# The end of an attention and MLP kernel: the last output tile in two PSUM banks, and half of the last squares on ScalarE

## The chip, the cores and the metric

One NeuronCore of one Trainium2 chip runs the whole program. The time is device microseconds of one execution. Three timed runs of the kernel before gave 680.88, 681.27 and 681.51 us, median 681.27 us. A separate execution was recorded by the profiler; it took 681.12 us, of which the span of the program's instructions is 679.3 us.

## The reference, cut to what matters

```python
# attention: softmax(scale * q k^T + bias(position)) v, for 4 batches, 8 heads, 576 positions, head size 64
attn_out = np.matmul(attn, v)                                  # 4 x 8 x 576 x 64
x = attn_out.transpose(0, 2, 1, 3).reshape(2304, 512)          # tokens x d_model
h = x @ w_in                                                   # 512 -> 2048
r = np.maximum(h, 0.0)
g = r * r
out = g @ w_out                                                # 2048 -> 512
```

All is float32. The change lies in the last three lines, for the last tokens that the kernel handles.

## The kernel before, in words

The attention comes first and leaves x in SBUF. The MLP follows as a list of 40 items `(n, P)`, in the order of the table `runs` (line 1299). A group n is a set of tokens; P is one of eight slices of the hidden size, 256 hidden units each. Groups 0 to 3 are the first 512 positions of one batch. Group `B` (4) holds what is left: the last 64 positions of each of the four batches, 256 tokens. It comes last, as items 32 to 39, and its products are 128 columns wide (`width[B]`).

One item goes through these functions. The loop runs item i's first half beside the second half of item i-1:

- `products` (L1416, TensorE): seven products of sums of quarters of x and w_in (Strassen's scheme), each in six matmuls of f16 parts. Four go to the PSUM tile `ha`, three to `hb`, 42 matmuls together.
- `sums` (L1430 to L1435): ScalarE scales `ha` into `s`; then VectorE puts the quarters of h together in `c`, in four operations: `c[2:4]`, `c[0:2]`, then twice `c[2:4]`, which alone needs `hb`.
- `squares` (L1452 for the late items): one VectorE operation makes max(c, 0) * c of the four quarters.
- `parts_g` (L1467, L1468): each hidden block f (0 or 1) is cut into two f16 parts. ScalarE makes `gh`, VectorE makes `gl`, the rest. Block f = 0 is `c[1]` and `c[3]`, block f = 1 is `c[0]` and `c[2]`.
- `down` (L1535, TensorE): the product with w_out. The output of group B is two tiles of 128 tokens and 512 columns, k = 0 and k = 1, each a whole PSUM bank (`y`), which adds up over all eight items. Per item, block f and tile k there are three matmuls: gh with the two parts of w_out (m = 0 and 1) and gl (m = 2). That makes 12. In the last item they are sorted by k.
- `leave` (L1498, L1501): when tile k is complete, VectorE copies it to SBUF with its scale (`o`), and two DMAs write it out, one half of the partitions (64 rows of 2 KB, one batch) from the SyncE queue, the other half from the ScalarE queue.

Each engine works through its instructions in the order in which the code issues them (`manual_schedule`); a DMA that is issued on ScalarE's queue stands among ScalarE's instructions. In tile k = 0, block 0 uses `c[3]` and block 1 uses `c[0]`; in tile k = 1 they use `c[1]` and `c[2]`. So `c[0:2]` holds one block of each of the two output tiles, and `c[2:4]` the other.

Of the kernel before, what the change touches and what calls it, by code (L numbers as in the profile page):

```python
# [10 lines left out]
F32 = mybir.dt.float32  # L11
F32R = mybir.dt.float32r
BF16 = mybir.dt.bfloat16
F16 = mybir.dt.float16
I32 = mybir.dt.int32
U32 = mybir.dt.uint32
AF = mybir.ActivationFunctionType
ALU = mybir.AluOpType
# [3 lines left out]
B, H, S, D = 4, 8, 576, 64  # L22
# [51 lines left out]
FINE = 1024.0  # L74
# [5 lines left out]
def attention_then_relu2_mlp(ctx: ExitStack, tc: tile.TileContext, q, k, v, cols, w_in, w_out, psi, xmat, dist, out):  # L80
    nc = tc.nc
    PE, DVE, ACT, POOL, SP = nc.tensor, nc.vector, nc.scalar, nc.gpsimd, nc.sync
# [668 lines left out]
    def take(x, o, n):  # L751
        o += 18 * S * x
        return area[:, o:o + n]
# [426 lines left out]
    order = [early[0], 2, 3, *early[1:]]  # L1180
# [113 lines left out]
    mlp = ctx.enter_context(tc.tile_pool(name="mlp", bufs=1, side="right", reuse_waits="tile"))  # L1294
    ph_p = ctx.enter_context(tc.tile_pool(name="ph", bufs=1, space=PSUM, reuse_waits="tile"))
    py_p = ctx.enter_context(tc.tile_pool(name="py", bufs=1, space=PSUM, reuse_waits="tile"))
# [4 lines left out]
    NI = len(items)  # L1301
    run_of = {(n, p0): r for r, (n, p0, p1) in enumerate(runs)}
    firsts = {(n, p0) for n, p0, p1 in runs}
    lasts = {(n, p1 - 1) for n, p0, p1 in runs}
# [19 lines left out]
    part_y, ready_y = {}, {}  # L1324
    c_t, g_t, y_t = {}, {}, {}
# [78 lines left out]
    def products(i):  # L1404
        n, P = items[i]
        w = width[n]
        ha = ph_p.tile([128, 4, 256], F32, name="ha", tag="ha")
        hb = ph_p.tile([128, 4, 256], F32, name="hb", tag="hb")
        for ms, h in (((2, 3, 4, 5), ha), ((1, 6, 7), hb)):
            for s, m in enumerate(ms):  # L1410
                k = 0
                for c in range(2):
                    wh, wl = (x[:, LEFT[m]] for x in w_t[4 * P + c])
                    xh, xl = (x[:, c] for x in xs_t[n, m])
                    for a, x in ((wh, xh), (wh, xl), (wl, xh)):
                        PE.matmul(h[:, s, :w], lhsT=a, rhs=x, start=(k == 0), stop=(k == 5))  # L1416
                        k += 1
        return ha, hb

    def sums(i, ha, hb):  # L1420
        n, P = items[i]
        w = width[n]
        alpha = alpha_t[n] if plain(n, P) else root[:, n:n + 1]
        if i % 2:
            c, s = (take(1, o, 1024).rearrange("p (m t) -> p m t", m=4)[:, :, :w] for o in (4480, 5504))
        elif i < NP // 2:
            c, s = (tmp_p.tile([128, 4, 256], F32, name=x, tag=x) for x in "cs")
        else:
            c, s = (xT[1][:, :, 256 * x:256 * x + w] for x in range(2))
        ACT.activation(out=s, in_=ha[:, :, :w], func=AF.Identity, scale=alpha)  # L1430
        stt = DVE.scalar_tensor_tensor
        stt(out=c[:, 2:4], in0=ha[:, 1:3, :w], scalar=alpha, in1=s[:, 0:4:3], op0=ALU.mult, op1=ALU.subtract)
        stt(out=c[:, 0:2], in0=ha[:, 2:4, :w], scalar=alpha, in1=s[:, 0:2], op0=ALU.mult, op1=ALU.add)  # L1433
        stt(out=c[:, 2:4], in0=hb[:, 0:1, :w].to_broadcast([128, 2, w]), scalar=alpha, in1=c[:, 2:4], op0=ALU.mult, op1=ALU.add)
        stt(out=c[:, 2:4], in0=hb[:, 1:3, :w], scalar=alpha, in1=c[:, 2:4], op0=ALU.mult, op1=ALU.add)  # L1435
        c_t[i] = c

    def squares(i):
        c = c_t[i]
        if i == 0:  # L1440
            for eng, f in ((DVE, 0), (ACT, 1)):
                g = c[:, 1 - f:4:2]
                if eng is DVE:
                    DVE.scalar_tensor_tensor(out=g, in0=g, scalar=0.0, in1=g, op0=ALU.max, op1=ALU.mult)
                else:
                    ACT.activation(out=g, in_=g, func=AF.Relu)
                    ACT.activation(out=g, in_=g, func=AF.Square)
        elif i < GA:
            ACT.activation(out=c, in_=c, func=AF.Relu)
            ACT.activation(out=c, in_=c, func=AF.Square)  # L1450
        else:
            DVE.scalar_tensor_tensor(out=c, in0=c, scalar=0.0, in1=c, op0=ALU.max, op1=ALU.mult)  # L1452

    def plain(n, P):
        return n < B - 1 and P < NP // 2

    def half(n, P, f):
        return not plain(n, P) and len(w_t[4 * P + 2 + f]) == 3

    def parts_g(i):  # L1460
        (n, P), c = items[i], c_t[i]
        w = width[n]
        for f in range(2):
            if half(n, P, f):
                gl, gh = (mlp.tile([128, 4, 256], F16, name=x, tag=x, bufs=2)[:, 0:2, :w] for x in ("gl", "gh"))
                g = c[:, 1 - f:4:2]
                ACT.activation(out=gh, in_=g, func=AF.Identity, scale=1.0 / FINE)  # L1467
                DVE.scalar_tensor_tensor(out=gl, in0=gh, scalar=-FINE, in1=g, op0=ALU.mult, op1=ALU.add)  # L1468
                g_t[i, f] = (gh, gl)
                continue  # L1470
            gl = mlp.tile([128, 2, 256], F32R, name="gl", tag="gl", bufs=2)[:, :, :w]
            gh = mlp.tile([128, 2, 256], F32R, name="gh", tag="gh", bufs=2)[:, :, :w]
            g = c[:, 1 - f:4:2]
            if plain(n, P):
                ACT.copy(gh, g)  # L1475
                DVE.tensor_tensor(out=gl, in0=g, in1=gh.bitcast(F32), op=ALU.subtract)
            else:
                ACT.activation(out=gh, in_=g, func=AF.Identity, scale=oscale[2])
                DVE.scalar_tensor_tensor(out=gl, in0=g, scalar=oscale[2], in1=gh.bitcast(F32), op0=ALU.mult, op1=ALU.subtract)
            g_t[i, f] = (gh, gl)  # L1480

    def pair_tile():
        return stage_p["p"].tile([128, 2, 512], F32, name="o", tag="stage", bufs=2)
# [8 lines left out]
    def leave(n, P, k):  # L1492
        y = y_t[n][k]
        j, x = divmod(k, 2)
        unit = 1.0 if plain(n, P) else beta[:, n:n + 1]
        if n == B:
            o = ready_y[j] = pair_tile()
            DVE.tensor_scalar(out=o[:, 0], in0=y, scalar1=unit, scalar2=None, op0=ALU.mult)  # L1498
            for r, queue in enumerate((SP, ACT)):
                end = S * (2 * k + r + 1)  # L1500
                queue.dma_start(out=out[end - 64:end], in_=o[64 * r:64 * r + 64, 0])  # L1501
            return
        if (n, 0) in part_y:
            o = ready_y[j]
            DVE.scalar_tensor_tensor(out=o[:, x], in0=y, scalar=unit, in1=o[:, x], op0=ALU.mult, op1=ALU.add)
        else:
            if x == 0:
                ready_y[j] = pair_tile()
            o = ready_y[j]
            ACT.activation(out=o[:, x], in_=y, func=AF.Identity, scale=unit)  # L1510
        if x == 0:
            return
        if P < NP - 1:
            ready_y[j, "dram"] = dram.tile([128, 1024], F32, name=f"py{j}")
            SP.dma_start(out=ready_y[j, "dram"], in_=o.rearrange("p x m -> p (x m)"))
        else:
            rows = out[S * n + 256 * j:S * n + 256 * j + 256].rearrange("(x p) m -> p x m", x=2)
            SP.dma_start(out=rows, in_=o)

    def down(i):  # L1520
        n, P = items[i]
        w = width[n]
        nk = w // 64
        if (n, P) in firsts:
            banks = {k: py_p.tile([128, 512], F32, name=f"y{k}") for k in (2, 3, 0, 1) if k < nk}
            y_t[n] = [banks[k] for k in range(nk)]
        order = [(f, k, m) for f in range(2) for ms in ((0, 1), (2,)) for k in range(nk) for m in ms]
        if i == NI - 1:
            order.sort(key=lambda x: x[1])
        for f, k, m in order:  # L1530
            wh, wl, *fine = w_t[4 * P + 2 + f]
            gh, gl = g_t[i, f]
            t, o = divmod(128 * k, w)
            slot = t if f else 1 - t
            PE.matmul(  # L1535
                y_t[n][k], lhsT=(gl if m == 2 else gh)[:, slot, o:o + 128], rhs=(wh, wl, *fine)[m] if fine else (wh, wl, wh)[m],
                start=((n, P) in firsts and f == 0 and m == 0), stop=((n, P) in lasts and f == 1 and m == 2),
            )
            if (n, P) in lasts and f == 1 and m == 2:
                leave(n, P, k)  # L1540
        if (n, P) in lasts and P < NP - 1:
            for j in range(2):
                part_y[n, j] = ready_y[j, "dram"]

    tmp_p = tmp_stack.enter_context(tc.tile_pool(name="tmp", bufs=1, side="right", reuse_waits="tile"))
    with tc.manual_schedule():
# [4 lines left out]
        for i in range(NI + 1):  # L1551
# [4 lines left out]
            n, P = items[min(i, NI - 1)]  # L1556
            if i:
                fetch_y(i - 1)
            if i < NI:
                ha, hb = products(i)  # L1560
# [9 lines left out]
            if i < NI:  # L1570
                sums(i, ha, hb)
# [35 lines left out]
            if i < NI and (n, P) in firsts:  # L1607
                r = run_of[n, P]
# [56 lines left out]
```

## Time and profile before

| | |
|---|---|
| timed runs, median (lowest to highest) | 681.27 us (680.88 to 681.51) |
| profiled execution / its span | 681.12 us / 679.3 us |
| TensorE matmul busy | 662.9 us, 98% |
| VectorE, ScalarE, GpSimd busy | 558.6, 484.9, 222.8 us |
| group B on TensorE, one item | 4.93 us (start to start) |
| end of the last matmul to the end of the span | 4.4 us |

Busy shares say which engine has work; what ends the program is read from the chain of waits, which goes back from the last instruction through whatever released each step. The span ends when the last output transfer has landed and the engines have met at the final barrier.

### The profile page before, as it was taken

The numbers are of one execution on the slowest core, as the hardware profiler recorded it, in microseconds if no ns is written. First come the engines' busy times: TensorE is split into PE (matmuls) and PEld (weight loads), VectorE is DVE, ScalarE is ACT, GpSimd is POOL, SyncE is SP. The second block draws the span as 40 slices with busy tenths as digits, with TensorE's granted clock in tenths as the row PEclk, the third lists the DMA queues.
The fourth block names the chain that finished last, engine by engine and source line by source line (L and its number), as shares of the span: only waits on it lengthen the run. The fifth ranks groups of instructions, "written<-read, shape, count | busy, mean of one in ns | idle before, by whom it ended". The sixth has DMA issues, their size and how long they took to land.

```text
span 679.3 us, 18939 instructions
## 1 busy us (share of the span) xinstructions
PE 662.9 (98%) x7650; PEld 509.4 (75%) x7650; DVE 558.6 (82%) x1216; ACT 484.9 (71%) x1013; POOL 222.8 (33%) x328
## 2 busy tenths in 40 slices
PE   9999999999999999899999999999999999999997
PEld 8788888887777777678888888887666666666664
DVE  7999899867779978998989879867758886798765
ACT  5779888888787999997566756775676657656321
POOL 2565545442112445455124205144212213331100
PEclk9999999999999999999999999999999999999999
DMA  6674210025073233306741040050038342633101
GB/s 200 196 248 138 94 65 3 2 88 151 11 242 104 52 115 110 104 4 220 292 171 64 32 171 32 5 229 0 1 106 316 110 153 109 226 131 121 66 2 32
DMA packets 34247, 76.67 MB, mean 113 GB/s; under 512 B 7152, under 2 KB 16496, under 8 KB 33136
## 3 DMA queue, kind: packets, MB, share of 16 engines
q1 hardware_dynamic: 34000, 75.21, 32.5%
q8 instruction: 60, 0.98, 0.6%
q14 instruction: 27, 0.22, 0.1%
q10 hardware_dynamic: 160, 0.26, 0.1%
HBM read 57.10 MB, written 18.35 MB: 111 GB/s over the span
## 4 chain that ended last, share of the span: by engine, by line
PE 71%; ACT 10%; DVE 7%; issue 4%; DMA 3%; POOL 3%; SPq 0%; ACTq 0%; POOLq 0%; DVEq 0%
PE y L1535 21%; PE sp L490 10%; PE px L623 10%; PE ha L1416 10%; PE hb L1416 7%; PE bb L430 6%; PE pp L571 4%; ACT pt L1259 3%; DMA r<-in_w_out 3%; ACT p L513 2%; DVE t L506 2%; PE pa L584 1%; POOL wa L804 1%; DVE area L906 1%; ACT o L1510 1%
## 5 line engine op out<-in xcount | busy, mean ns | idle before, releaser
L1416 PEld LDWEIGHTS <-area 128*128 128x128 f16 x1680 | 149.3, 98 | 24.4 <-issue 2.4
L1535 PE MATMUL y<-w,gh 128*128 128x512 f16 (+1 forms) x576 | 142.9, 387 | 0.7 <-ACT gh L1475 0.3
L506 DVE CUSTOM_DVE_ANT_0 t<-sp,area 128x576 f32<-128x576 f32 x144 | 103.7, 752 | 18.7 <-PE sp L490 9.6
L513 ACT ACTIVATE p<-t,negm 128x576 f32<-128x576 f32 x144 | 113.2, 799 | 1.1 <-DVE negm L506 0.9
L490 PE MATMUL sp<-k,q 64*128 64x288 f32 (+1 forms) x608 | 94.7, 427 | 2.6 <-DVE negm L506 1.6
L623 PE MATMUL px<-pt,v 128*64 128x128 f32 (+1 forms) x1600 | 92.2, 266 | 1.2 <-ACT pt L1259 1.2
L623 PEld LDWEIGHTS px<-pt,v 128*64 128x64 f32 x1600 | 79.2, 137 | 12.1 <-ACT pt L1259 8.6
L1416 PE MATMUL ha<-area 128*128 128x256 f16 (+1 forms) x816 | 84.9, 260 | 0.2 <-DVE area L1433 0.2
L445 POOL TENSOR_TENSOR area<-bt,bt 128x256 f32<-128x256 f32 x72 | 65.7, 929 | 55.6 <-DVE bt L438 55.4
L1535 PE MATMUL y<-w,gl 128*128 128x512 f16 (+1 forms) x288 | 77.0, 384 | 0.0
L490 PEld LDWEIGHTS sp<-k,q 64*128 64x128 f32 (+1 forms) x608 | 50.1, 177 | 21.1 <-issue 6.0
L1416 PE MATMUL hb<-area 128*128 128x256 f16 (+1 forms) x612 | 64.7, 260 | 0.0
L833 POOL TENSOR_TENSOR raw<-wa 128x256 f32<-128x256 f32 (+1 forms) x48 | 31.3, 679 | 88.7 <-issue 54.1
L1535 PEld LDWEIGHTS <-gh 128*128 128x128 f16 x344 | 33.1, 98 | 35.6 <-ACT gh L1467 1.1
L417 DVE TENSOR_TENSOR mask<-sdist,theta 128x1024 f16<-128x1024 f16 x81 | 58.0, 718 | 1.1 <-PE bb L430 0.8
L571 PEld LDWEIGHTS pp<-ident,p 64*128 64x128 f32 x1144 | 45.5, 139 | 13.9 <-issue 1.9
L982 ACT COPY pt<-pp 128x512 f32<-128x512 f32 (+1 forms) x76 | 37.4, 544 | 21.5 <-PE pp L571 21.4
L571 PE MATMUL pp<-ident,p 64*128 64x64 f32 x1144 | 50.1, 226 | 2.2 <-DVE raw L832 0.7
L1535 PEld LDWEIGHTS y<-w,gh 128*128 128x128 f32 x232 | 42.5, 188 | 10.2 <-ACT gh L1475 1.0
L430 PEld LDWEIGHTS <-mask 128*128 128x128 f16 x1296 | 46.3, 100 | 4.1 <-issue 1.6
L430 PE MATMUL bb<-wmov,mask 128*128 128x64 f16 x1296 | 47.3, 194 | 0.2 <-ACT pt L982 0.2
L1259 ACT COPY pt<-pp 128x512 f32<-128x512 f32 (+1 forms) x83 | 39.8, 563 | 10.8 <-PE pp L571 10.4
(231 smaller groups left out, 1103.8 us busy)
## 6 DMA issues: line engine op xcount, KB each, us to landing
raw<-in_w_in SPq DMA_DIRECT2D x20, 512.0 KB, 3.9
r<-in_w_out SPq DMA_DIRECT2D x16, 512.0 KB, 7.4
xs<-area SPq DMA_DIRECT2D x4, 1792.0 KB, 9.1
area<-in_w_in SPq DMA_DIRECT2D x12, 512.0 KB, 4.4
py<-o SPq DMA_DIRECT2D x12, 512.0 KB, 4.1
o<-py SPq DMA_DIRECT2D x12, 512.0 KB, 4.3
v<-in_v SPq DMA_DIRECT2D x16, 320.0 KB, 3.3
q<-in_q SPq DMA_DIRECT2D x32, 128.0 KB, 3.5
```

The source lines that it names most:

```text
L417: DVE.tensor_tensor(out=out, in0=win, in1=th, op=ALU.is_ge)
L430: PE.matmul(bb[:, 64 * (7 - r):64 * (8 - r)], lhsT=m[:, r], rhs=wmov[:, n], start=(n == 0), stop=(n == 1))
L445: POOL.tensor_tensor(out=dst, in0=tw, in1=sw, op=ALU.add)
L490: mm = PE.matmul(out_t[to, x, :HALF], lhsT=lhsT, rhs=rhs, start=True, stop=True)
L506: DVE.tensor_tensor_reduce(out=t.rearrange("p (x n) -> p x n", x=2), in0=sp[:, :, :HALF], in1=bias.rearrange("p (x n) -> p x n", x=2), sca ...
L513: ACT.activation(out=p[:, S * n:S * n + S], in_=t, func=AF.Exp, bias=negm[:, n:n + 1], scale=-1.0, accum_out=sums[:, 2 * ic + n:2 * ic + n ...
L571: PE.transpose(dst, p[rows, k0:k0 + 128], ident[rows, rows])
L623: PE.matmul(px[64 * h:64 * h + 64, 128 * m:128 * m + w], lhsT=vt[:, c, h], rhs=src, start=(c == 0), stop=(c == 4))
L982: ACT.copy(dst, src)
L1259: ACT.copy(*c)
L1416: PE.matmul(h[:, s, :w], lhsT=a, rhs=x, start=(k == 0), stop=(k == 5))
L1535: PE.matmul(y_t[n][k], lhsT=(gl if m == 2 else gh)[:, slot, o:o + 128], rhs=(wh, wl, *fine)[m] if fine else (wh, wl, wh)[m], start=((n, P) ...
```

## The change

Three things are changed for group B. First, tile k = 1 lies in two banks: its columns 0 to 255 in one, 256 to 511 in another, so each of its matmuls becomes two of 256 columns, in all eight items. When it is complete, VectorE copies the first half and ScalarE the second, and each half goes out as one DMA of 128 rows of 1 KB, from the SyncE and the ScalarE queue. Second, in the last item `c[0:2]` is summed first and then squared by ScalarE in two activations (Relu, Square); VectorE squares `c[2:4]` alone; `gh` and `gl` are cut in the same halves. Third, the last item's matmuls are ordered by those halves: all that use `c[0:2]` first, then the others, tile 0 before tile 1.

```diff
 def sums(i, ha, hb):
         ACT.activation(out=s, in_=ha[:, :, :w], func=AF.Identity, scale=alpha)
+        if i == NI - 1:
+            stt(out=c[:, 0:2], in0=ha[:, 2:4, :w], scalar=alpha, in1=s[:, 0:2], op0=ALU.mult, op1=ALU.add)
+            ACT.activation(out=c[:, 0:2], in_=c[:, 0:2], func=AF.Relu)
+            ACT.activation(out=c[:, 0:2], in_=c[:, 0:2], func=AF.Square)
         stt(out=c[:, 2:4], in0=ha[:, 1:3, :w], scalar=alpha, in1=s[:, 0:4:3], op0=ALU.mult, op1=ALU.subtract)
-        stt(out=c[:, 0:2], in0=ha[:, 2:4, :w], scalar=alpha, in1=s[:, 0:2], op0=ALU.mult, op1=ALU.add)
+        if i < NI - 1:
+            stt(out=c[:, 0:2], in0=ha[:, 2:4, :w], scalar=alpha, in1=s[:, 0:2], op0=ALU.mult, op1=ALU.add)
...
 def squares(i):
-        if i == 0:
+        if i == NI - 1:
+            DVE.scalar_tensor_tensor(out=c[:, 2:4], in0=c[:, 2:4], scalar=0.0, in1=c[:, 2:4], op0=ALU.max, op1=ALU.mult)
+        elif i == 0:
...
 def parts_g(i):
+        if i == NI - 1:
+            gl, gh = (mlp.tile([128, 4, 256], F16, name=x, tag=x, bufs=2)[:, :, :w] for x in ("gl", "gh"))
+            for x in (slice(0, 2), slice(2, 4)):
+                ACT.activation(out=gh[:, x], in_=c[:, x], func=AF.Identity, scale=1.0 / FINE)
+            for x in (slice(0, 2), slice(2, 4)):
+                DVE.scalar_tensor_tensor(out=gl[:, x], in0=gh[:, x], scalar=-FINE, in1=c[:, x], op0=ALU.mult, op1=ALU.add)
+            g_t[i, 0], g_t[i, 1] = ((gh[:, 1 - f:4:2], gl[:, 1 - f:4:2]) for f in range(2))
+            return
...
 def leave(n, P, k):
+        if n == B and k:
+            o = ready_y[j] = pair_tile()
+            rows = out[2 * S * k:2 * S * k + 2 * S].rearrange("(r s) m -> r s m", r=2)[:, S - 64:]
+            DVE.tensor_scalar(out=o[:, 0, :256], in0=y[0], scalar1=unit, scalar2=None, op0=ALU.mult)
+            ACT.activation(out=o[:, 0, 256:], in_=y[1], func=AF.Identity, scale=unit)
+            for x, queue in enumerate((SP, ACT)):
+                queue.dma_start(out=rows[:, :, 256 * x:256 * x + 256], in_=o[:, 0, 256 * x:256 * x + 256])
+            return
...
 def down(i):
-            banks = {k: py_p.tile([128, 512], F32, name=f"y{k}") for k in (2, 3, 0, 1) if k < nk}
+            banks = {k: py_p.tile([128, 512], F32, name=f"y{k}") for k in (2, 3, 0, 1) if k < nk + (n == B)}
             y_t[n] = [banks[k] for k in range(nk)]
+            if n == B:
+                y_t[n][1] = [banks[k][:, :256] for k in (1, 2)]
...
-            order.sort(key=lambda x: x[1])
+            order.sort(key=lambda x: (x[0] == x[1], x[2] == 2 and x[0] != x[1], x[1]))
...
+            if n == B and k:
+                for x, y in enumerate(y_t[n][k]):
+                    PE.matmul(y, lhsT=lhsT, rhs=rhs[:, 256 * x:256 * x + 256], start=start, stop=stop)
+            else:
+                PE.matmul(y_t[n][k], lhsT=lhsT, rhs=rhs, start=start, stop=stop)
```

TensorE's last instructions before the change, from the start of the last item's second half: `y_10289` is output tile 0 and `y_10290` tile 1; `w_9378` and `w_9472` are the w_out parts of the hidden blocks 0 and 1; names in brackets are the engines waited for.

```order
L1535 LDWEIGHTS gh [waits Activation_49]
L1535 MATMUL y_10289<-w_9378,gh 128x512
...
L1535 LDWEIGHTS gl [waits DVE_49]
L1535 MATMUL y_10289<-w_9472,gl 128x512
L1535 LDWEIGHTS gh
L1535 MATMUL y_10290<-w_9378,gh 128x512
...
L1535 LDWEIGHTS gl
L1535 MATMUL y_10290<-w_9472,gl 128x512
```

Tile 0 is complete when six matmuls of tile 1 are still to come.

The same place after the change, from the second half of that item on: `y_10290` is now tile 0, `y_10291` and `y_10289` are the two halves of tile 1.

```order
L1567 LDWEIGHTS gl [waits DVE_49]
L1567 MATMUL y_10290<-w_9472,gl 128x512
...
L1567 LDWEIGHTS gh [waits Activation_49]
L1567 MATMUL y_10290<-w_9378,gh 128x512
...
L1567 LDWEIGHTS gl [waits DVE_49]
L1567 MATMUL y_10290<-w_9378,gl 128x512
L1565 LDWEIGHTS gh
L1565 MATMUL y_10291<-w_9472,gh 128x256
L1565 LDWEIGHTS gh
L1565 MATMUL y_10289<-w_9472,gh 128x256
```

The `c[0:2]` half and the `c[2:4]` half each have their own waits on ScalarE and VectorE, and tile 0 is complete three full matmuls' worth before the end, where it was six.

ScalarE's last instructions before the change:

```order
L1430 ACTIVATE area<-ha,xT_83 128x4x128 [waits PE_49]
L1467 ACTIVATE gh<-area 128x2x128 [waits DVE_49,PE_49,Activation_49]
L1467 ACTIVATE gh<-area 128x2x128 [waits PE_49,Activation_49]
L1501 DMA out<-o 64x512 [waits DMAHW3_49,DVE_49]
L1501 DMA out<-o 64x512 [waits DMAHW5_49,DVE_49]
```

And after it:

```order
L1430 ACTIVATE area<-ha,xT_83 128x4x128 [waits PE_49]
L1434 ACTIVATE area<-area 128x2x128 [waits DVE_49]
L1435 ACTIVATE area<-area 128x2x128 [waits Activation_49]
L1473 ACTIVATE gh<-area 128x2x128 [waits PE_49,Activation_49]
L1473 ACTIVATE gh<-area 128x2x128 [waits DVE_49]
L1524 DMA out<-o 64x512 [waits DMAHW3_49,DVE_49]
L1515 ACTIVATE o<-y_10289,xT_83 128x256 [waits DMAHW4_49,DMAHW2_49,DMAHW6_49,DMAHW1_49,DMAHW7_49,DMAHW0_49,PE_49]
L1517 DMA out<-o 2x64x256 [waits Activation_49]
```

ScalarE's copy of the last half tile stands behind the issue of tile 0's DMA, which waits for VectorE's copy of tile 0.

## Rows read from the trace of the kernel before

**Rows 1.** The page: the span, and the busy time of each engine.

```profile
span 679.3 us, 18939 instructions
PE 662.9 (98%) x7650; PEld 509.4 (75%) x7650; DVE 558.6 (82%) x1216; ACT 484.9 (71%) x1013; POOL 222.8 (33%) x328
```

**Rows 2.** Chain that ended last, in time: start us, us, what.

```profile
664.33 2.59 PE y L1535 x12
...
668.30 0.70 ACT area L1430
...
669.02 0.48 DVE area L1432
...
669.81 0.48 DVE area L1434
...
670.84 0.70 DVE area L1452
...
671.65 0.42 ACT gh L1467
...
672.12 2.80 PE y L1535 x12
...
674.95 0.75 DVE o L1498
```

**Rows 3.** TensorE's timeline at the end: start us, us, what, count, idle before.

```profile
671.26 0.59 PE L1535 MATMUL y<-w,gl 128*128 128x512 f16 x2
672.12 0.61 PE L1535 MATMUL y<-w,gh 128*128 128x512 f16 x2 [0.26 <-ACT gh L1467]
...
673.24 0.38 PE L1535 MATMUL y<-w,gl 128*128 128x512 f16 x1
...
674.53 0.38 PE L1535 MATMUL y<-w,gl 128*128 128x512 f16 x1
```

**Rows 4.** The timeline from 674.40 and from 675.65 us, all engines; SPq and ACTq are issues.

```profile
673.65 0.75 DVE L1498 TENSOR_SCALAR o<-y,xT 128x512 f32<-128x512 f32 x1 [0.80 <-PE y L1535]
...
674.43 0.52 SPq L1501 DMA_DIRECT2D out<-o  x1
674.44 0.57 ACTq L1501 DMA_DIRECT2D out<-o  x1
...
675.73 0.49 SPq L1501 DMA_DIRECT2D out<-o  x1
675.73 0.51 ACTq L1501 DMA_DIRECT2D out<-o  x1
```

**Rows 5.** TensorE's timeline where products are 256 columns wide.

```profile
600.19 2.78 PE L1416 MATMUL ha<-area 128*128 128x256 f16 x24
602.81 0.38 PE L1416 MATMUL hb<-area 128*128 128x256 f16 x2
```

**Rows 6.** Groups of the page: weight loads, mean ns of one.

```profile
L1535 PEld LDWEIGHTS <-gh 128*128 128x128 f16 x344 | 33.1, 98 | 35.6 <-ACT gh L1467 1.1
```

**Rows 7.** Groups by shape, ScalarE, 580 to 679.3 us: busy us, mean ns | idle before.

```profile
L1467 ACT ACTIVATE gh<-area 128x256 f16<-128x256 f32 x8 | 2.9, 408 | 11.2 <-DVE area L1452 11.2
L1430 ACT ACTIVATE area<-ha,xT 128x512 f32<-128x512 f32 x4 | 2.8, 688 | 4.3 <-PE ha L1416 4.3
L1430 ACT ACTIVATE area<-ha,xT 128x1024 f32<-128x1024 f32 x3 | 3.3, 1108 | 3.3 <-PE ha L1416 3.3
```

**Rows 8.** VectorE's timeline, 636 to 640 us: four copies of output tiles in a row.

```profile
636.70 2.73 DVE L1505 SCALAR_TENSOR_TENSOR o<-y,xT,o 128x512 f32<-128x512 f32 x4 [1.19 <-PE y L1535]
```

**Rows 9.** Line L1501: issues and waits (ns min/median/max, first and last start), landing.

```profile
L1501 ACTq EVENT_SEMAPHORE  x2: 17/17/17, 671.8 to 675.0; - x2
...
DMA to landing us min/median/max: 2.4/2.5/2.7
```

**Rows 10.** All output DMAs of 600 to 682 us (tile out).

```profile
L1518 SPq DMA_DIRECT2D out<-o x6: 388/388/389, 601.2 to 639.5; - x6
...
DMA to landing us min/median/max: 2.4/2.8/3.0
```

More of the change, by code (lines that the diff above doesn't have):

```diff
@@ L1524, in down @@
         if (n, P) in firsts:
-            banks = {k: py_p.tile([128, 512], F32, name=f"y{k}") for k in (2, 3, 0, 1) if k < nk}
+            banks = {k: py_p.tile([128, 512], F32, name=f"y{k}") for k in (2, 3, 0, 1) if k < nk + (n == B)}
             y_t[n] = [banks[k] for k in range(nk)]
+            if n == B:
+                y_t[n][1] = [banks[k][:, :256] for k in (1, 2)]
         order = [(f, k, m) for f in range(2) for ms in ((0, 1), (2,)) for k in range(nk) for m in ms]
         if i == NI - 1:
-            order.sort(key=lambda x: x[1])
+            order.sort(key=lambda x: (x[0] == x[1], x[2] == 2 and x[0] != x[1], x[1]))
+        ended = {k: (f, m) for f, k, m in order}
         for f, k, m in order:
@@ L1534, in down @@
             slot = t if f else 1 - t
[L1535 to L1539, printed above, removed]
+            lhsT, rhs = (gl if m == 2 else gh)[:, slot, o:o + 128], (wh, wl, *fine)[m] if fine else (wh, wl, wh)[m]
+            start, stop = (n, P) in firsts and f == 0 and m == 0, (n, P) in lasts and ended[k] == (f, m)
+            if n == B and k:
[3 more added lines that the diff above has]
+                PE.matmul(y_t[n][k], lhsT=lhsT, rhs=rhs, start=start, stop=stop)
+            if (n, P) in lasts and ended[k] == (f, m):
                 leave(n, P, k)
```

## The prediction

> **What bounds the kernel now.** I read the page first: the span is 679.3 us and TensorE is busy for 662.9 of them [rows 1]. That only says that nothing but TensorE can matter through most of the program. The change touches the last 40 us, so the view that decides is the chain of waits at its end [rows 2]. The reader is to see there that one item of group B follows the other on TensorE without a break until 669 us, and that the chain then leaves TensorE for the last item's sums: ScalarE's scaling at 668.30, VectorE's four sums and its square up to 671.54, ScalarE's `gh` at 671.65, twelve matmuls from 672.12, and VectorE's copy of tile 1 at 674.95. TensorE's timeline shows the price of that detour: two matmuls of the item before started at 671.26, and the first of the last item at 672.12 [rows 3]. Last I read the issues: both queues issue tile 1's DMAs at 675.73 [rows 4], and 3.57 us later the span ends. Everything that the change can win lies between 671.7 and 675.73.
>
> **TensorE, the split.** Matmuls of 512 columns follow each other every 2.59 / 12 = 0.216 us [rows 2]; those of 256 columns, each with its own weight load, every (602.81 - 600.19) / 24 = 0.109 us [rows 5]. A pair of halves costs 2 x 0.1092 - 0.2158 = 0.0025 us more than the one it replaces. Six pairs an item, eight items, makes 48 pairs and 0.12 us; 42 pairs (0.105 us) lie ahead of the last item's matmuls. The lower bound is nothing; the upper one is a case of its own below.
>
> **TensorE, the wait.** The two matmuls of 671.26 leave a free place at 671.26 + 2 x 0.216 = 671.69; the last item takes it at 672.12, so 0.43 us are lost (the view says 0.26, since a matmul's end is drawn later than the next one's start). After the change the place is free at 671.69 + 0.105 = 671.80. Are the early halves there? `c[0:2]` is now the first sum, done at 669.02 + 0.48 + 0.09 (36 pairs lie before it) = 669.59. Relu, Square and `gh` on 256 elements follow on ScalarE, which is idle there: the nearest row is 0.41 us [rows 7], bounds 0.41 and 0.69 (512 elements). Three of them with the hand-overs end at 670.94, at the upper bound at 671.75. Both are in time, so the work moved to ScalarE costs nothing. VectorE's square of `c[2:4]` is 256 elements instead of 512; `gh[2:4]` is ready at about 672.0 and `gl[2:4]` at 672.45, and TensorE asks for them at 673.10 and 673.54. No stall is left: the wait is gone.
>
> **TensorE, the end.** From 671.80: six early places 1.30, tile 0's three 0.65, tile 1's six halves 0.655, so the stream ends at 674.40. A matmul is drawn to its end 0.16 us after that (0.38 against 0.216 [rows 3]): tile 0 is complete at 673.91, tile 1's halves at 674.46 and 674.57. Before, tile 0 was complete at 673.62 and tile 1 at 674.91. So TensorE ends 0.34 us earlier, but tile 0 comes 0.29 us later.
>
> **The copies and the issues.** This is where the sum turns. VectorE copies tile 0 from 673.95 to 674.70 (0.75 [rows 4]). It can begin the next copy one step later, 2.73 less 0.75, over three steps = 0.66 us [rows 8], at 674.61, and a copy of 256 elements from PSUM takes 0.48 (the sums, [rows 2]): 675.09. SyncE's queue has issued tile 0's half by 674.74 + 0.52 = 675.26 and can issue again then. That path is 0.47 us earlier than before.
>
> ScalarE's path is not. Its copy stands behind its own issue of tile 0's DMA, which waits for VectorE's copy: 674.74 to 675.31 (0.57 [rows 4]). The trace of before has no computing instruction behind an issue on ScalarE, but its second wait at L1501 starts only at 675.0 [rows 9], when the first issue ends. I take it that ScalarE starts nothing before 675.31. Then come waits for six DMA queues, three instructions of 17 ns or more with gaps, bounds 0 and 0.2, I take 0.12: 675.43. The copy: 688 ns at 512 elements and 1108 at 1024 [rows 7] make 0.42 per 512, so 0.48 at 256; bounds 0.41 and 0.69 from the rows of 256 from SBUF and 512 from PSUM. It ends at 675.91, and the DMA is issued at 675.94. That is 0.21 us later than the 675.73 of before.
>
> The Trainium skill (Perfetto Trace Analysis, section DMA Instruction — HWDGE) says the same against this change: the time shown for an issue runs until the sequencer is free for its next instruction. The waits of [rows 9] agree with it. The skill's table in VectorE: DVE Perf Modes (section on the TRN2 errata) gives ScalarE 172 cycles plus one per element from PSUM; by it the copy would be an estimated 0.36 us and the sum 0.12 lower, but at 512 elements it would say 0.57 where [rows 7] have 0.69.
>
> **The landing.** ScalarE's half goes out as 128 rows of 1 KB instead of 64 of 2 KB, alone on the engines by then. No row has this form. From issue to landing the rows have 2.4 to 2.7 [rows 9] and, for four times the bytes, up to 3.0 [rows 10]; issues took 0.39 to 0.57. I take the 2.7 of before, so that the rest of the span stays 3.57 us. Bounds: 0.3 earlier or later.
>
> **The sum.** 675.94 + 3.57 = 679.51 for the span, 0.21 us more: 681.12 + 0.21 = 681.33 for the profiled execution. The timed runs' median lies 0.15 above the profiled one, so 681.48, given as 681.5. With every unknown at its lower bound (issue 0.39, no waits, copy 0.41, landing 0.3 shorter) the sum is 0.46 lower than before, where SyncE's path, 0.47 earlier, leaves it; with every upper bound it is 0.8 higher. That is 680.8 to 682.1, and 680.6 to 682.2 with what runs differ by (0.3 either way). A measurement of this kernel tells a change from none at about 0.2%, 1.36 us; none of this reaches it.
>
> **The rivals.**
>
> *The gain passes through (0.25).* If an issue on ScalarE's queue doesn't hold its copy, the copy runs from 674.61 to 675.09, and ScalarE issues again as soon as its first issue ends, at 675.31: 0.42 earlier, 680.85. For it: issues aren't counted as busy time of the engine. Against it: the wait at 675.0 [rows 9].
>
> *The change doesn't do what it says (0.07).* `gh` of the last item is now one tile in place of two; if the first matmul waits until all of it is written, TensorE starts at about 672.07 as before, tile 0 leaves 0.27 later still, and ScalarE's DMA goes out at 676.21: 0.48 later than before, 681.75. Against it: the new order has a wait of its own for each half.
>
> *Slower: the split (0.03).* If the second half of each pair doesn't hide its weight load, each of the 48 pairs costs up to 0.098 us [rows 6] more, on TensorE, which is the chain here [rows 2]: 4.7 us, 686.0. From 0.024 us a pair on (1.15 us on top of 681.48) it passes 0.2%. Against it: in [rows 5] every matmul of 256 columns has a load of its own and still goes at 0.109.
>
> *The forecast (0.65):* 681.5.
>
> **How the numbers follow.** The forecast and the first two rivals, 0.97 together, all lie within 0.2% of 681.27; I leave 0.02 of them for a faster and 0.02 for a slower measurement, and add the split's 0.03 to the slower. Faster 0.02, same 0.93, slower 0.05. The range of 680.6 to 682.2 takes in the passing gain and the missing early half; only the split is outside.
>
> **What would show it.** In the profile after: matmuls of group B at 256 columns every 0.109 us, items 4.94 us apart where they were 4.93; the last item's first matmul right behind the one before, near 671.8, with no idle time; the last matmul's end near 674.57; VectorE's copy of tile 0 near 673.95; on ScalarE the copy L1515 starting 0.1 us or so after the issue L1524 ends, near 675.4, and its DMA at 675.9 as the last issue, 0.7 us behind SyncE's. A copy L1515 that starts at 674.6 would prove the first rival, idle time before 672.1 the second, a longer step between items the third. The forecast's sign is wrong if the last issue comes before 675.7 or a half tile of 1 KB rows lands in much less than 2.6 us.

## The result and the profile after

The changed kernel takes 686.22 us (median of six runs, 684.96 to 686.50), the kernel before 681.39 us (six runs, 680.88 to 681.58). The ratio is 1.0071, interval 1.006 to 1.0081: slower by 4.8 us, or 0.7%. The prediction was 681.5 us with a range up to 682.2, and a chance of 0.05 for slower by more than 0.2%. It was wrong.

The page of the changed kernel, its span and busy times. Read it against [rows 1]: TensorE's busy time is the same to 0.1 us, the span is 5.1 us longer.

```profile
span 684.4 us, 19038 instructions
PE 663.0 (97%) x7698; PEld 514.4 (75%) x7698; DVE 557.9 (82%) x1216; ACT 486.2 (71%) x1016; POOL 222.8 (33%) x328
```

TensorE's timeline of the changed kernel at the end, which answers to [rows 3]; L1565 are the halves of 256 columns, L1567 the full matmuls.

```profile
671.68 0.38 PE L1565 MATMUL y<-w,gl 128*128 128x256 f16 x2
671.90 0.59 PE L1567 MATMUL y<-w,gh 128*128 128x512 f16 x2
...
674.29 0.38 PE L1565 MATMUL y<-w,gl 128*128 128x256 f16 x2
```

There is no idle time before 671.90 any more, and the last matmul ends at 674.67, where it was 674.91. TensorE did what was forecast. The timeline of all engines after that answers to [rows 4]; L1521 copies tile 0 and L1524 issues its DMAs, L1514 and L1515 copy the halves of tile 1 and L1517 issues theirs:

```profile
674.05 0.75 DVE L1521 TENSOR_SCALAR o<-y,xT 128x512 f32<-128x512 f32 x1 [1.49 <-PE y L1567]
...
674.72 0.48 DVE L1514 TENSOR_SCALAR o<-y,xT 128x256 f32<-128x256 f32 x1
674.83 0.52 SPq L1524 DMA_DIRECT2D out<-o  x1
674.84 0.61 ACTq L1524 DMA_DIRECT2D out<-o  x1
675.40 0.65 SPq L1517 DMA_DIRECT2D out<-o  x1
675.72 0.47 ACT L1515 ACTIVATE o<-y,xT 128x256 f32<-128x256 f32 x1 [3.62 <-DVE o L1514]
676.23 1.08 ACTq L1517 DMA_DIRECT2D out<-o  x1
```

The last issue stands at 676.23, 0.5 us after the 675.73 of before. But from there to the end of the span it is 8.2 us, where it was 3.6. The time went after the last issue, into the output DMA itself. The windows show how (us from the span's start; at the end of each line granted clock, DMA share, GB/s). First the kernel before, which moves nothing more after 678.0 (its last landing is near 678.4, 2.7 us after the issue at 675.73 [rows 9]):

```profile
677.00:678.00 1.00, 0.00 (x0) 0.00 (x0) 0.00 (x0) 0.00 (x0) 0.00 (x0) 1.00 0.87 234
678.00:679.00 1.00, 0.00 (x0) 0.00 (x0) 0.00 (x0) 0.00 (x0) 0.00 (x0) 0.77 0.00 0
```

Then the changed one:

```profile
678.00:679.00 1.00, 0.00 (x0) 0.00 (x0) 0.00 (x0) 0.00 (x0) 0.00 (x0) 0.85 0.14 49
679.00:680.00 1.00, 0.00 (x0) 0.00 (x0) 0.00 (x0) 0.00 (x0) 0.00 (x0) 0.50 0.13 47
...
681.00:682.00 1.00, 0.00 (x0) 0.00 (x0) 0.00 (x0) 0.00 (x0) 0.00 (x0) 0.50 0.13 47
682.00:683.00 1.00, 0.00 (x0) 0.00 (x0) 0.00 (x0) 0.00 (x0) 0.00 (x0) 0.50 0.13 46
```

A flat share of 0.13 to 0.14 for six microseconds is close to 2 / 16, what it would be if two of the 16 DMA engines worked, at 47 GB/s together. The queues' packets of the last ten microseconds of the changed kernel point the same way (packets, MB, share; q1 is SyncE's queue, q10 ScalarE's):

```profile
q1 hardware_dynamic: 210, 0.26, 10.2%
q10 hardware_dynamic: 210, 0.26, 6.9%
```

Before, each queue had 160 packets there: twice 64 rows and 16 small ones. Now it is 64 + 16 for tile 0 and 130 for tile 1: 128 rows and two small ones. The DMA of tile 1 writes `rows`, a view of two batches by 64 rows, so its outer dimension is 2. The Trainium skill states the rule (DMA: Bandwidth & Descriptors, section Rules for kernel authors): the slowest dimension that isn't 1 decides over how many engines a DMA is spread, and an outermost one of fewer than 16 confines all of it to at most that many. The share of 0.13 and the two small packets agree with it. I had not weighed it. Whether this is the cause, and whether it is all, was tried.

### The profile page after: what moved, and what is told of

It is laid out like the page before. It is cut to its first block, busy times and chain, and to the rows that moved or that the text cites. A ratio compares the mean times of both kernels' runs of the same rounds, so it can differ in the third digit from the quotient of the medians.

```text
span 684.4 us, 19038 instructions
## 1 busy us (share of the span) xinstructions
PE 663.0 (97%) x7698; PEld 514.4 (75%) x7698; DVE 557.9 (82%) x1216; ACT 486.2 (71%) x1016; POOL 222.8 (33%) x328
## 4 chain that ended last, share of the span: by engine, by line
PE 73%; ACT 10%; DVE 9%; issue 4%; POOL 3%; DMA 0%; DVEq 0%; ACTq 0%; POOLq 0%
PE y L1567 19%; PE ha L1416 10%; PE px L623 10%; PE sp L490 10%; PE hb L1416 7%; PE bb L430 6%; PE pp L571 4%; ACT pt L1259 3%; ACT p L513 2%; DVE t L506 2%; PE y L1565 1%; PE pa L584 1%; POOL wa L804 1%; DVE wa L224 1%; DVE wa L223 1%
## 5 line engine op out<-in xcount | busy, mean ns | idle before, releaser
L1567 PE MATMUL y<-w,gh 128*128 128x512 f16 (+1 forms) x544 | 135.6, 388 | 0.5 <-ACT gh L1490 0.3
L1567 PE MATMUL y<-w,gl 128*128 128x512 f16 (+1 forms) x272 | 73.3, 384 | 0.0
L1567 PEld LDWEIGHTS <-gh 128*128 128x128 f16 x312 | 30.1, 98 | 29.5 <-ACT gh L1482 0.3
L1567 PEld LDWEIGHTS y<-w,gh 128*128 128x128 f32 x232 | 42.5, 188 | 10.2 <-ACT gh L1490 1.0
```

Source lines behind the costliest of these rows:

```text
L1567: PE.matmul(y_t[n][k], lhsT=lhsT, rhs=rhs, start=start, stop=stop)
```

## The experiments

Three theories. A: the outer dimension of 2 puts the DMA on two engines. B: rows of 1 KB, or two queues writing into the same 2 KB rows, are slow. C: ScalarE's late copy is what costs.

**The DMA in pieces of 64 rows.** Edit on the changed kernel:

```diff
             for x, queue in enumerate((SP, ACT)):
-                queue.dma_start(out=rows[:, :, 256 * x:256 * x + 256], in_=o[:, 0, 256 * x:256 * x + 256])
+                for r in range(2):
+                    queue.dma_start(out=rows[r, :, 256 * x:256 * x + 256], in_=o[64 * r:64 * r + 64, 0, 256 * x:256 * x + 256])
```

> The changed kernel with one edit: each half of tile 1 goes out as two DMAs of 64 rows of 1 KB (one per batch) on its queue, instead of one DMA of 2 x 64 rows. Theory A (a DMA whose outer dimension is 2 is carried by two of the 16 DMA engines; the trace after shows a DMA share of 0.13 to 0.14 and 47 GB/s for six microseconds): the share goes back up, each DMA lands 2.4 to 2.8 us after its issue, the last issue on ScalarE's queue is one issue (0.55 us) later, at about 676.8, so the span is about 680.4 us and the time about 682.3 us, 4 us less than the 686.2 of the changed kernel. Theory B (rows of 1 KB are slow to write, or the two queues hinder each other in the same 2 KB rows): nothing is gained, 686 to 687 us. Theory C (the late ScalarE copy is what costs): the copy stays late, so 686 us as well.

Measured 681.76 us, ratio to the kernel before 1.0005 (0.9996 to 1.0014). The rows are still 1 KB, written by two queues, and ScalarE's copy is as late as before the edit. The DMA view of the last microseconds (KB each, median us from issue to landing):

```profile
out<-o SPq DMA_DIRECT2D x2, 64.0 KB, 2.2
out<-o ACTq DMA_DIRECT2D x2, 64.0 KB, 2.2
```

So B is not the cause, and C is not the cause of the 4.8 us. This kernel is not told apart from the kernel before.

**The DMA alone, on the kernel before.** Edit in `leave`, nothing else of the change:

```diff
+            if k:
+                rows = out[2 * S * k:2 * S * k + 2 * S].rearrange("(r s) m -> r s m", r=2)[:, S - 64:]
+                for x, queue in enumerate((SP, ACT)):
+                    queue.dma_start(out=rows[:, :, 256 * x:256 * x + 256], in_=o[:, 0, 256 * x:256 * x + 256])
+                return
```

> The kernel before with one edit: tile 1 is copied as before by VectorE alone, but goes out as two DMAs of 2 x 64 rows of 1 KB, columns 0 to 255 from SyncE's queue and 256 to 511 from ScalarE's. No bank is split, no square is moved, no copy is on ScalarE. Theory A: 256 KB at 47 GB/s take 5.6 us from about 1.6 us after the issue of 675.73, so the last landing is near 683, the span 684 and the time about 685.8 us. Theory B: slower as well, by an amount it does not give. Theory C: the time is that of the kernel before, 681.4 us.

Measured 686.45 us, ratio 1.0072 (1.0058 to 1.0086): all the loss of the change, with this line of it alone.

**One DMA of whole rows.** As above, but with one line `SP.dma_start(out=rows, in_=o[:, 0])`.

> The kernel before with one edit: tile 1 goes out as one DMA of 2 x 64 whole rows of 2 KB from SyncE's queue, where it had one DMA of 64 rows on each of two queues. Theory A: the outer dimension is 2, so the same 256 KB go through two engines, about 47 GB/s, and the time is about 685.8 us, DMA share 0.13. Theory B (rows of 1 KB, or two queues in the same rows): neither is there, so about 681.4 us.

Measured 686.80 us, ratio 1.0079 (1.0065 to 1.0092). Neither small rows nor two queues are needed. Both kernels are somewhat slower than expected, by 0.7 and 1.0 us.

**Half the bytes.** On the kernel before: SyncE's queue has the DMA of 2 x 64 rows of 1 KB, ScalarE's queue writes the other columns in two DMAs of 64 rows.

```diff
...
+                SP.dma_start(out=rows[:, :, 0:256], in_=o[:, 0, 0:256])
+                for r in range(2):
+                    ACT.dma_start(out=rows[r, :, 256:], in_=o[64 * r:64 * r + 64, 0, 256:])
...
```

> The kernel before with one edit: of tile 1 only the columns 0 to 255 go out as one DMA of 2 x 64 rows of 1 KB (SyncE's queue); the columns 256 to 511 go out as two DMAs of 64 rows of 1 KB (ScalarE's queue). Half as many bytes through the form with the outer dimension 2 as in the two-column kernel (686.45 us) and the one-DMA kernel (686.80 us). Theory A, two engines at 47 GB/s: 128 KB take 2.8 us instead of 5.6, so the time is about 683.7 us. The rival, a fixed delay for every DMA of this form whatever its size: about 686.5 us again.

Measured 684.20 us, ratio 1.0045 (1.0032 to 1.0059). The loss goes with the bytes, 2.9 us against 5.0 and 5.4; it is not a fixed delay. It is 0.5 more than expected. One of the two DMAs of 64 rows on ScalarE's queue landed only 4.0 us after its issue, where DMAs of this form took 2.1 to 2.3 in the first kernel above; that they share the two engines with SyncE's DMA would explain it, but was not tried. The landing of those two (line L1503):

```profile
DMA to landing us min/median/max: 1.9/3.0/4.0
```

**Another outer dimension.** The kernel before, with tile 1 as one DMA to an aside buffer; the 128 rows of the output that it holds are left unwritten. With outer dimension 16 the numbers are `a=16` and `:8`.

```diff
...
+                aside = dram.tile([256, 512], F32, name="aside")
+                SP.dma_start(out=aside.rearrange("(a t) m -> a t m", a=4)[:, :32], in_=o[:, 0])
...
```

> The kernel before with one edit: tile 1 goes out as one DMA of 256 KB from SyncE's queue, in rows of 2 KB, to an aside buffer in HBM (256 rows, of which 4 groups of 32 are written), so that the DMA's outer dimension is 4. The 128 rows of the output that tile 1 holds are left unwritten. It is the one-DMA kernel (outer dimension 2, 686.80 us) with another outer dimension. Theory A in its general form, as many engines as the outer dimension says: four engines at about 94 GB/s, 2.8 us of transfer instead of 5.6, the landing 2.8 us earlier, so about 684.0 us, and 4 small packets beside the 128 rows. If 2 were a special case (two batches, or any outer dimension over the rows): 686.8 us, or 681.4.

> The same with 16 groups of 8 rows: the outer dimension is 16, all else as in the kernel with 4 groups; the 128 rows of the output that tile 1 holds are left unwritten. Theory A in its general form: all 16 engines, 0.7 us of transfer, landing 2.4 to 2.8 us after the issue, about 681.5 us, and 16 small packets. If any DMA whose rows fall into groups is slow: 686.8 us.

Measured 684.61 us (ratio 1.0054, 1.0038 to 1.007) with 4, 0.6 us more than expected, and 681.63 us (1.0008, 0.9997 to 1.0019) with 16. One window of each of the three kernels, late in the big DMA, while it alone runs (DMA share and GB/s at the end of the line); outer dimension 2:

```profile
681.00:682.00 1.00, 0.00 (x0) 0.00 (x0) 0.00 (x0) 0.00 (x0) 0.00 (x0) 0.50 0.13 49
```

Outer dimension 4:

```profile
679.00:680.00 1.00, 0.00 (x0) 0.00 (x0) 0.00 (x0) 0.00 (x0) 0.00 (x0) 0.50 0.26 98
```

Outer dimension 16:

```profile
677.40:678.20 0.80, 0.00 (x0) 0.00 (x0) 0.00 (x0) 0.00 (x0) 0.00 (x0) 1.00 0.93 236
```

The share is about 2/16, then 4/16, then nearly all 16, and the rate doubles from 49 to 98 GB/s with the second pair of engines. The first microseconds of the two narrow DMAs are slower: 35 and 27 GB/s from 678 to 680 us with outer dimension 2, 27 and 84 from 677 to 679 with 4. This goes with the times above the expected ones; why the start is slow stays open. SyncE's queue has 210, 212 and 224 packets at the end of the three kernels: 80 for tile 0, 128 rows, and 2, 4 and 16 small ones. Theory A holds in its general form, for the four outer dimensions tried (2, 4, 16 and 64).

**The change without the fault.** On the changed kernel, tile 1 goes out as before, by batch, when both halves are copied:

```diff
-            for x, queue in enumerate((SP, ACT)):
-                queue.dma_start(out=rows[:, :, 256 * x:256 * x + 256], in_=o[:, 0, 256 * x:256 * x + 256])
+            for r, queue in enumerate((SP, ACT)):
+                queue.dma_start(out=rows[r], in_=o[64 * r:64 * r + 64, 0])
```

> The changed kernel with one edit: when both halves of tile 1 are copied, it goes out as before, as one DMA of 64 rows of 2 KB from each queue. All else of the change stays: two banks, two copies, squares, order. This is the change as the prediction imagined it. By the trace after, ScalarE's copy ends 9.25 us after the last item's first matmul, where the last issue of the kernel before stands at 8.97; both issues at 9.28, landing 2.4 to 2.7 us later, end of the span at 12.9 against 12.57, plus 0.1 us of split before that: 681.8 us, about 0.4 over the kernel before. The first rival of the prediction (the gain passes through) says 680.9.

Measured 681.62 us, ratio 1.0013 (1.0003 to 1.0023): the rest of the change costs a little, as the prediction had it. The interval only just leaves out no change; in the trace the span ends 0.27 us later than before, counted from the last item's first matmul. ScalarE's timeline of this kernel shows why: its copy begins only 0.28 us after its own issue of tile 0's DMA has ended.

```profile
674.49 0.57 ACTq L1524 DMA_DIRECT2D out<-o  x1
675.34 0.47 ACT L1515 ACTIVATE o<-y,xT 128x256 f32<-128x256 f32 x1 [3.57 <-DVE o L1514]
675.84 0.50 ACTq L1517 DMA_DIRECT2D out<-o  x1
```

**Squares and order alone.** The changed kernel without two banks, ScalarE's copy and the new DMAs (`leave` and the banks of `down` as before).

> The changed kernel without its first part: tile 1 stays in one bank, is copied by VectorE alone and goes out by two DMAs of 64 rows of 2 KB as before; the squares on ScalarE and the new order of the last item's matmuls stay. All theories on the DMA: none of the 5 us is left. The prediction's own steps say that TensorE's wait of 0.43 us goes: last matmul done near 674.48, VectorE's copy of tile 1 can start 0.66 us after that of tile 0 (673.85), at 674.51, and both DMAs are issued near 675.29, 0.44 us before the 675.73 of the kernel before: 680.95 us. The rival (tile 0 now comes late and VectorE's two copies get in each other's way) says no gain, 681.4 us.

Measured 681.35 us, ratio 1.0002 (0.9991 to 1.0014): no gain that the runs can tell, where 0.44 us was expected. In its trace the last issues stand 8.52 us after the last item's first matmul, 0.45 earlier than before, as worked out. But the span is only 0.15 us shorter from that point. Its timeline has the issues of tile 1:

```profile
674.79 0.50 SPq L1516 DMA_DIRECT2D out<-o  x1
674.79 0.78 ACTq L1516 DMA_DIRECT2D out<-o  x1
```

And the landing of the four DMAs of line L1516:

```profile
DMA to landing us min/median/max: 2.4/2.5/3.0
```

ScalarE's queue had ended its issue for tile 0 just 0.1 us before. This issue takes 0.78 instead of 0.51 [rows 4], and a DMA lands as late as 3.0 us after its issue, where 2.7 was the most [rows 9].

**Tile 0 first.** Two kernels with one other sort in `down`: on the squares and order alone, and on the change without the fault.

```diff
-            order.sort(key=lambda x: (x[0] == x[1], x[2] == 2 and x[0] != x[1], x[1]))
+            order.sort(key=lambda x: (x[1], x[0] == x[1]))
```

> The squares and the order alone (one bank, VectorE copies, DMAs as before), with the last item's matmuls sorted by tile and within a tile the half that ScalarE squared first. In the kernel with squares and order alone the last issue came 0.45 us earlier than before, but ScalarE's queue had ended its issue of tile 0 only 0.1 us before; that second issue took 0.78 us instead of 0.51 and landed 2.99 us after its start instead of 2.63, which gave 0.36 back. Theory D (that crowding of the two issues): with tile 0 complete 0.65 us earlier the issue is 0.51 long again, lands after 2.63 us, and the time is 680.95 us. The rival (the 2.99 is the chance of one execution): as the other kernel, about 681.3 us by the clock on the wall, and a landing that is not tied to the distance of the issues.

Measured 680.56 us, ratio 0.9993 (0.9984 to 1.0002). TensorE has no wait here either. The issues of tile 1:

```profile
674.67 0.49 SPq L1516 DMA_DIRECT2D out<-o  x1
674.68 0.51 ACTq L1516 DMA_DIRECT2D out<-o  x1
```

The latest landing is at 2.7 us again. With 0.7 us between the two issues of ScalarE's queue all is as before, and the span is 0.44 us shorter from the last item's first matmul on. So two tiles that go out close together do cost something, with one trace of each kernel; what crowds is not separated. In the kernel with squares and order alone the data of the two tiles also move without a pause (DMA share 0.86, 1.08 and 0.87 in the three half microseconds from 675.5), where the share falls to 0.50 between them here. And closeness of issues alone doesn't fix the price: on ScalarE's queue a second issue 0.03 us after another took 0.85 us in the kernel with pieces of 64 rows, and one 0.04 us after another took 0.61 in the kernel with half the bytes.

> As the changed kernel with DMAs of 64 rows of 2 KB, and with the last item's matmuls sorted by tile, within a tile the half that ScalarE squared first. TensorE still has no wait (gl of c[2:4] is asked for 1.08 us after the item's first matmul and is ready 0.6 us after it), and tile 0 is complete after six of twelve matmuls, at about 6.4 us, so ScalarE's issue of its DMA ends near 7.8 and no longer holds ScalarE's copy: both copies of tile 1 end by 8.25, the issues stand at 8.28 instead of 8.97, the span ends 0.69 earlier less 0.1 for the split: 680.8 us. If instead an issue soon after another on the same queue is slow (0.78 instead of 0.51, landing 3.0 instead of 2.63, as in the kernel with squares and order alone), 0.3 of it is given back: 681.1.

Measured 680.99 us, ratio 0.9993 (0.9978 to 1.0007). ScalarE's copy now waits for TensorE and not for an issue:

```profile
673.54 0.57 ACTq L1524 DMA_DIRECT2D out<-o  x1
674.38 0.47 ACT L1515 ACTIVATE o<-y,xT 128x256 f32<-128x256 f32 x1 [2.92 <-PE y L1565]
674.89 0.51 ACTq L1517 DMA_DIRECT2D out<-o  x1
```

Both are the fastest versions tried, their medians 0.7 and 0.3 us below that of the kernel before in the same set of runs (681.25). The intervals of both still take in 1, so a gain isn't shown by the timed runs; the traces, one of each, have 0.44 and 0.39 us from the last item's first matmul on.

## Why the prediction was wrong, step by step

Times from the last item's first matmul (666.76 before, 666.95 after), so that nothing ahead of it enters; the predicted ones are the prediction's, less 666.85. In the last row the spans are not rounded (679.33 and 684.43 us), where the prediction took 679.3.

| | before | predicted | after |
|---|---|---|---|
| first matmul of the last `down` | 5.36 | 4.95 | 4.95 |
| tile 0 complete, VectorE's copy begins | 6.89 | 7.10 | 7.10 |
| last matmul's end | 8.15 | 7.72 | 7.72 |
| ScalarE's copy begins | | 8.58 | 8.77 |
| last issue | 8.97 | 9.09 | 9.28 |
| from the last issue to the end of the span | 3.60 | 3.57 | 8.20 |

**The split** was right: four halves take 0.44 us from 673.85 to 674.29, 0.11 each, and the items' start-to-start step is 4.95 us instead of 4.93, much as six pairs at 0.0025 would have it.

```profile
662.00 1.50 PE L1416 MATMUL ha<-area 128*128 128x128 f16 x24
...
666.95 1.50 PE L1416 MATMUL ha<-area 128*128 128x128 f16 x24
...
673.85 0.60 PE L1565 MATMUL y<-w,gh 128*128 128x256 f16 x4
```

The rival in which the second half shows its weight load gave 686.0 us, and the time came out there, but by another mechanism: no pair is longer, and the two-column DMA on the kernel before, where nothing is split, has the whole loss.

**The wait and the end on TensorE** were right to 0.01 us: the wait went, tile 0 came late. That also refutes the second rival, which kept the wait.

**The copies and the issues** were right in kind. ScalarE's copy did stand behind its own issue: it begins at 675.72, and the issue before it ends at 675.45. That refutes the first rival, in which the gain passes through. Two terms were small: the three waits took 0.28 us instead of 0.12, the issue 0.61 instead of 0.57. Together that is the 0.19 us by which the last issue is later than predicted. ScalarE's copy of 256 elements took 0.475 us; the prediction's 0.48 from [rows 7] was right, and the estimate of 0.36 by the Trainium skill's table (VectorE: DVE Perf Modes, section on the TRN2 errata) was too low.

**The landing** is the step that failed. The prediction said that no row had this form, and then bounded it by [rows 9, 10] at 2.4 to 3.0 us, with 0.3 either way. All those rows have an outer dimension of 64 or 128 and bounded nothing for a DMA with an outer dimension of 2, which uses about 2/16 of the DMA engines' time instead of nearly all. The form stood in the new order (2x64x256), and the count of rows per DMA was noticed; the count of engines was not. Nor was ScalarE's half alone on the engines, as the prediction had it: from 679 to 682 us both queues move packets (63 and 79), at a share of 0.13 to 0.14 together, and the 256 KB of both halves went through at 47 GB/s. From the last issue to the end of the span it measured 8.20 us, 4.6 more than the 3.57 taken, and that is nearly the whole of the 4.8 us.

**The forecast without that step** was 681.5 us; the change without the fault measures 681.62. Runs of one kernel differ by 0.3 us and more, so this bears out the rest of the sum, but not to a tenth.

## What to carry to other kernels

Look at the outer dimension of every DMA that is cut anew: two batches of 64 rows as one DMA went out at a share of 2/16 and 47 GB/s, and as DMAs of 64 rows it cost nothing that the runs can tell, for one more issue on each queue, of 0.6 us on SyncE's and 0.85 on ScalarE's. A bound from the nearest rows holds only if those rows share what decides the cost; where a row of a new form is missing, say in what it differs and price each difference. And before a copy goes to an engine that also issues DMAs, see what stands ahead of it in that engine's order. Here, in one trace of each kernel and counted from the last item's first matmul, moving tile 0 forward shortened the end by 0.29 us without the split and by 0.66 with it, while splitting tile 1 lengthened it by 0.42 with the change's order and 0.05 with tile 0 first.

## What the runs showed of the hardware that I had not expected

- One DMA of 256 KB to HBM with an outer dimension of 2, 4 and 16 ran at a DMA share of 0.13, 0.26 and 0.93, and at 49, 98 and 236 GB/s, each in a window late in the DMA. If the share counts engines, that is an estimated 24 GB/s for each engine while two or four are in use, and 15 for each of the 16.
- The issue of such a DMA is longer too: 0.65 us on SyncE's queue and 1.08 and 1.26 on ScalarE's for two groups of 64 rows, where 64 rows took 0.48 to 0.61 apart from the two issues close behind another on ScalarE's queue (0.78 and 0.85).
- An issue on ScalarE's queue 0.1 us after another took 0.78 us and landed after 3.0; 0.7 us after it, 0.51 and at most 2.7. On SyncE's queue the same closeness cost nothing in that kernel (0.50), and on ScalarE's one issue 0.04 us behind another took 0.61, so the cause stays open.
- Waits for six DMA queues in front of one ScalarE instruction took 0.28 us in three instructions, though the DMA share had been 0.00 from 665 to 676 us:

```profile
L1515 ACTq EVENT_SEMAPHORE  x3: 38/38/38, 675.5 to 675.6; - x3
```
